# Loads of xn^T and x tied to one copy of the attention gradient, and two transposes of w_v moved behind the last dh1 transposes

## The chip, the cores and the metric

The kernel runs on one core of one Trainium2 chip. The time is device microseconds of one execution; several executions are timed and the median is given. The engines are named as in the profile: PE (TensorE matmul), PEld (its weight loads), DVE (VectorE), ACT (ScalarE), POOL (GpSimd) and SP (SyncE). SP issues the DMA transposes and the plain loads of one hardware queue (q1 in the profile), POOL issues plain copies through a software queue (q0). All matrices are bfloat16, all matmul sums fp32.

## What is computed

One transformer block (pre-LN linear attention with 32 heads of 20, then pre-LN SwiGLU) over 2048 tokens of width 640 and a hidden width of 1728, and its gradients with respect to x and all five weight matrices.

```python
def _A_ref(x, wqkv, wo):
    qkv = (x @ wqkv).reshape(B, S, 3, H, Dh).transpose(2, 0, 3, 1, 4)
    q, k, v = qkv[0], qkv[1], qkv[2]
    phi = lambda t: jnp.where(t > 0, t + 1, jnp.exp(t)) + 1e-6
    pq, pk = phi(q), phi(k)
    kv = jnp.einsum("bhsd,bhse->bhde", pk, v)
    z = jnp.einsum("bhsd->bhd", pk)
    num = jnp.einsum("bhqd,bhde->bhqe", pq, kv)
    den = jnp.einsum("bhqd,bhd->bhq", pq, z)[..., None] + 1e-6
    return (num / den).transpose(0, 2, 1, 3).reshape(B, S, D) @ wo
def _B_ref(x, w_gate, w_up, w_down):
    return (jax.nn.silu(x @ w_gate) * (x @ w_up)) @ w_down
h  = x + _A_ref(_layernorm(x), A_wqkv, A_wo)
h2 = h + _B_ref(_layernorm(h), B_w_gate, B_w_up, B_w_down)
out, vjp = jax.vjp(f, A_x, A_wqkv, A_wo, B_w_gate, B_w_up, B_w_down)
return (out, *vjp(grad_out))
```

## The kernel before

Tokens lie in 16 tiles of 128 rows ("token 14" below is tile 14 of 0 to 15), a width of 640 is five blocks of 128. The stages, with rough times in the span of the profile: layer norm and k, q (to 51 us), linear attention forward (to 139), the SwiGLU gradient in four column groups (to 436), the gradient through the second layer norm together with the gradient of the attention output (436 to 586), then the weight gradients of attention and dx (586 to 722), and the block's output (to the end).

The change sits in the stage from 436 to 586 us and in the code behind it. This stage is a loop over p (two tokens a turn) that works on three pairs of tokens at once. For the pair p the matmuls of d hn2 run (`ps_dhd`, `ps_dhc`, `ps_dha`). For the pair v = p - 1 the layer-norm gradient ends in dh1 (`ln_add`), and `tr_dh1` has SP transpose dh1 of each token by DMA into a buffer called `stg`, the odd token first. For the pair q = p - 2, with tokens u0 = 2q and u1 = 2q + 1, `dp_mm` multiplies that transposed dh1 with W2^T on PE into `ps_dp`, `dp_copy` copies it on ACT into `dq`, and DVE works on it. Three `stg` buffers are in turn: token 14's transpose writes the one that `dp_mm` of token 13 reads, and the first two row loads of pk (`pkr`) take the next turns.

In the turn p = 8, called `last` in the code, there is no pair left for d hn2, and PE fills its time with part sums of GT = dh1^T pq (`ps_gt`) for rows whose dh1 is ready. In the turn p = 9 only the pair 14 and 15 is left: `dp_mm(14)`, twelve `ps_gt` matmuls, `dp_mm(15)`. Then come two more blocks of `ps_gt`, `ps_dz`, the weight gradient `dwqk` (which reads x, normalised again in place in `hn`, there also called `xn_r`), `ps_dkvt`, `wk2` (which reads the transposed w_v), `ps_dk` (which reads xn^T, `xnT_r`) and `ps_dxn` (which reads the transposed w_q and w_k, and a ring of transposes).

The transposes on SP around that place are: five of w_o (`woT`, in turn 7), in turn 8 four column blocks of w_v by `tr_cols` into `wqkvT[:, 10 + j]`, then `tr_dh1` of tokens 15 and 14, then two more column blocks of w_v and ten of w_q and w_k. POOL, in turns 3, 5, 7 and 9, issues `load_xr4(c)`, which loads four tokens of x into `hn`, and after the loop four loads of xn^T, each of 640 KB, from the copy that the forward pass left in DRAM.

The stage stands in a `manual_schedule` of all engines, so the written order is the order of issue. `tc.issue_after(late)` in the part behind it only tells the scheduler where in the order an instruction may stand; it makes no semaphore. `late` is the `dp_copy` of the even token of the latest turn, in the end that of token 14. `wait_for(on, dmas)` (lines 216 to 219) adds a true dependency, so that the issuing queue waits on a semaphore until the instruction `on` has ended.

Of the kernel before, what the change touches and what calls it, by code (L numbers as in the profile page):

```python
# [20 lines left out]
def kernel(  # L21
# [8 lines left out]
    nc = tc.nc  # L30
# [18 lines left out]
    x_v = A_x.rearrange("b (t p) d -> p (b t) d", p=P)  # L49
# [16 lines left out]
    def row(ps):  # L66
        return ps[:, :, :320]

    def half(ap):
        return ap.rearrange("p (c n) -> p c n", c=2)  # L70
# [10 lines left out]
    scr_xnT = dram.tile([ST, P, DT, P], BF16, name="scr_xnT")  # L81
# [32 lines left out]
    HG = len(OH)  # L114
# [44 lines left out]
    def pool_load(out, in_):  # L159
        nc.gpsimd.dma_start(out=out, in_=in_)  # L160
# [54 lines left out]
    def wait_for(on, dmas):  # L215
        info = mybir.DependencyInfo(mybir.DependencyClass.Sync, mybir.DependencyReason.DATA)
        for dma in dmas:
            tc.add_manual_dep(dma.ins, on.ins.name, info, reason="paced")
# [266 lines left out]
    with tc.manual_schedule(engines={EngineType.PE, EngineType.DVE, EngineType.SP, EngineType.Pool}):  # L485
# [41 lines left out]
        hn = big.tile([P, ST, D], BF16, name="hn", tag="B")  # L527
# [410 lines left out]
    with tc.manual_schedule(engines=ALLE):  # L938
# [102 lines left out]
        def tr_cols(dst, src, c):  # L1041
            nc.sync.dma_start_transpose(out=dst.unsqueeze(1), in_=src[:, c:c + P])
# [3 lines left out]
        def get_wqkvT():  # L1046
            if not wqkvTs:
                wqkvTs.append(big.tile([P, 16, D], BF16, name="wqkvT", tag="B"))
            return wqkvTs[0]
# [19 lines left out]
        def dqv(t):  # L1069
            return dq[t // 8][:, t % 8, :]  # L1070
# [3 lines left out]
        def dp_mm(t):  # L1074
            pdp[t] = mm("ps_dp")
            d = dh1Ts.pop(t)
            mm_row(pdp[t], lambda i: d[:, i, :], lambda i, n0, n1: W2T[:, i, n0:n1], DT)

        def dp_copy(t):
            return nc.scalar.copy(out=half(dqv(t)), in_=row(pdp.pop(t)))  # L1080

        def dp_pr(t):
            tt(pr[:], dqv(t), pqs_tm[:, t, :], ALU.mult)
# [9 lines left out]
        def dp_end(t):  # L1093
            s = rw[t][:]
            tt(s, s, zb[:], ALU.mult)
            tt(dqv(t), dqv(t), s)
            tt(dqv(t), dqv(t), Eb[t][:], ALU.mult)
# [17 lines left out]
            nc.gpsimd.dma_start(out=out_6[j * P:min(j * P + P, F), :], in_=dwds.pop(j)[:min(P, F - j * P), :])  # L1115

        def load_xr4(c):
            nc.gpsimd.dma_start(out=hn[:, 4 * c:4 * c + 4, :], in_=x_v[:, 4 * c:4 * c + 4, :])

        gts = {}  # L1120

# [32 lines left out]
        for p in range(1, NPR + 2):  # L1154
            v, q = p - 1, p - 2
            e0, o0 = 2 * v, 2 * v + 1
            u0, u1 = 2 * q, 2 * q + 1
# [5 lines left out]
                for b in (*rws, *Ebs, pr):  # L1163
                    nc.gpsimd.memset(b[:, 0:1], 0.0)
            if last:
                for j in range(4):
                    tr_cols(get_wqkvT()[:, 10 + j, :], A_wqkv, 2 * D + OH[j])
            if run:
                load_pq(p)
# [59 lines left out]
                for i in range(3):  # L1229
                    gt_part(gts[i], i, ST - 2, ST)  # L1230
            if dpq:
                late = dp_copy(u0).ins
                dp_pr(u0)
                dp_mm(u1)
            if first:
# [40 lines left out]
            if run:  # L1276
                ln_mul(2 * p + 1)
            if p >= 3 and p % 2 == 1:
                with tc.issue_after(late):
                    load_xr4((p - 3) // 2)  # L1280
        dp_end(ST - 1)

    with tc.manual_schedule(engines={EngineType.SP, EngineType.DVE}):
# [3 lines left out]
        xnT_r = big.tile([P, ST, DT, P], BF16, name="xnT_r", tag="B")  # L1287
# [3 lines left out]
        def load_pk(t):  # L1291
            pkrs[t] = small.tile([P, D], BF16, name="pkr", tag="stg", bufs=3, padded_shape=[P, 7 * P])
            pool_store(pkrs[t][:], scr_pk_v[:, t, :])

        load_pk(0)
        load_pk(1)
        for j in range(4, HG):
            with tc.issue_after(last_dh1T):
                tr_cols(wqkvT[:, 10 + j, :], A_wqkv, 2 * D + OH[j])
        for k in (0, 1):  # L1300
# [1 line left out]
                with tc.issue_after(last_dh1T):  # L1302
                    tr_piece(wqkvT[:, 5 * k:5 * k + 5, :], A_wqkv[:, k * D:(k + 1) * D], i)
        for c in range(4):
            with tc.issue_after(late):
                pool_load(xnT_r[:, 4 * c:4 * c + 4], scr_xnT[4 * c:4 * c + 4].rearrange("t p k c -> p t k c"))

        GT = mat(2 * DT * D, DT, D)
        for i in range(DT):
# [51 lines left out]
        for r in range(4):  # L1361
            for ci, (n0, n1) in enumerate(NCH):
                for j in range(4):
                    t = 4 * r + j
# [302 lines left out]
```

## Time and profile before

| what | us |
|---|---|
| median of 3 runs | 792.43 |
| the runs | 790.3, 792.43, 800.54 |
| the profiled execution, its own time | 792.55 |
| its span, first to last instruction | 790.8 |
| PE busy in the span | 777.3 |
| DVE, ACT, POOL busy | 590.6, 347.7, 180.8 |

The span is what the engines' instructions cover; 1.75 us of the profiled execution's time lie around it. PE is busy for 98% of it, so the kernel is bounded by matmuls nearly everywhere, and what PE waits for is what can be had. The mean granted clock of TensorE is 0.994.

### The profile page before, as it was taken

To read this page: it belongs to the slowest core of one execution; us is meant where nothing else is said; L and a number is where in the kernel's file an instruction comes from. 1 tells how busy PE (TensorE), PEld (TensorE's weight loads), DVE (VectorE), ACT (ScalarE), POOL (GpSimd) and SP (SyncE) were. 2 spreads that over 40 slices of the span, in tenths; PEclk is the share of its full clock that TensorE was granted. 3 is DMA by queue.
4 is the path that set the end of the run, shared out by engine and by line. 5 is a ranking of instruction groups with operands and counts; after the bars stand their busy time and mean duration, and the time that the engine had idled before them with its cause. 6 is when DMAs were issued, how large, how long until landed. Compare 5 with 4: busy or idle time off the path is not lost.

```text
span 790.8 us, 14151 instructions
## 1 busy us (share of the span) xinstructions
PE 777.3 (98%) x5462; PEld 518.6 (66%) x5462; DVE 590.6 (75%) x1041; ACT 347.7 (44%) x545; POOL 180.8 (23%) x310
## 2 busy tenths in 40 slices
PE   9999999999999999999999999999969999999998
PEld 7676566556655665566666777777647777777776
DVE  7979988898697868776979379988843366634873
ACT  6962532762284145423831457766622133334010
POOL 4600037511201120012322222242201111123210
PEclk9999999999999999999999999999979999999999
DMA  9799999999679898892797699896984899999992
GB/s 261 163 238 302 201 226 261 274 243 229 190 164 220 183 228 191 215 241 80 158 232 232 212 221 241 224 274 123 204 193 113 151 149 183 177 172 315 236 203 89
DMA packets 288420, 162.37 MB, mean 205 GB/s; under 512 B 241548, under 2 KB 277197, under 8 KB 288352
## 3 DMA queue, kind: packets, MB, share of 16 engines
q1 hardware_dynamic: 269120, 101.25, 63.4%
q0 software_dynamic: 16608, 56.65, 24.0%
q10 hardware_dynamic: 2624, 3.56, 1.5%
q8 instruction: 43, 0.70, 0.4%
q14 instruction: 25, 0.20, 0.1%
HBM read 47.60 MB, written 53.66 MB: 128 GB/s over the span
## 4 chain that ended last, share of the span: by engine, by line
PE 90%; DVE 6%; DMA 3%; issue 1%; ACT 0%; POOL 0%; SPq 0%; ACTq 0%; DVEq 0%
PE ps_dxn L1430 8%; PE ps_wa L648 7%; PE pg L828 6%; PE pu L833 6%; PE ps_dwqk L1342 6%; PE ps_dm L422 5%; PE ps_qd L648 5%; PE ps_dha L991 5%; PE ps_oa L1507 4%; PE ps_kq L309 4%; PE ps_wc L648 3%; PE ps_dk L108 3%; PE ps_y L515 3%; PE ps_a L578 3%; PE ps_dw L684 3%; PE ps_dp L108 3%
## 5 line engine op out<-in xcount | busy, mean ns | idle before, releaser
L828 PE MATMUL pg<-wgu,hnT 128*128 128x448 bf16 (+1 forms) x320 | 64.1, 346 | 0.0
L833 PE MATMUL pu<-wgu,hnT 128*128 128x448 bf16 (+1 forms) x320 | 63.6, 346 | 0.0
L1430 PEld LDWEIGHTS <-ring 128*128 128x128 bf16 x480 | 46.9, 98 | 18.5 <-DMA ring<-dq 0.4
L1430 PE MATMUL ps_dxn<-wqkvT,ring 128*128 128x320 bf16 x320 | 51.3, 299 | 0.0
L833 PEld LDWEIGHTS <-hnT 128*128 128x128 bf16 x320 | 31.3, 98 | 27.1
L828 PEld LDWEIGHTS <-hnT 128*128 128x128 bf16 x320 | 31.3, 98 | 26.0
L422 PEld LDWEIGHTS <-dh2T 128*128 128x128 bf16 x320 | 31.0, 98 | 25.1
L422 PE MATMUL ps_dm<-wdT,dh2T 128*128 128x448 bf16 (+1 forms) x240 | 46.5, 344 | 0.0
L309 PE MATMUL ps_kq<-wqk,xnT 128*128 128x320 bf16 x320 | 44.8, 299 | 0.4 <-DMA xnT<-xn 0.4
L648 PEld LDWEIGHTS <-S 128*128 128x128 bf16 x320 | 30.9, 98 | 21.1 <-DVE dd L644 0.2
L849 ACT ACTIVATE dd<-pg 128x896 bf16<-128x896 f32 (+1 forms) x32 | 28.5, 891 | 28.9 <-PE pg L828 28.9
L309 PEld LDWEIGHTS <-xnT 128*128 128x128 bf16 x320 | 30.9, 98 | 12.9 <-DMA xnT<-xn 0.7
L1342 PEld LDWEIGHTS <-hn 128*128 128x128 bf16 x320 | 31.0, 98 | 12.1 <-issue 0.3
L873 POOL DMA_DIRECT2D scr_m<-m_s x16 | 12.2, 759 | 110.3 <-DVE m_s L860 110.3
L648 PE MATMUL ps_wa<-dd,hn 128*128 128x448 bf16 (+1 forms) x192 | 37.0, 346 | 0.0
L146 DVE CUSTOM_DVE_ANT_0 lb_a<-lb_dy,hn 128x640 bf16<-128x640 bf16 x16 | 13.2, 826 | 30.5 <-ACT lb_dy L144 30.5
L860 DVE TENSOR_TENSOR m_s<-m_s,dd 128x896 bf16<-128x896 bf16 (+1 forms) x32 | 19.3, 604 | 21.4 <-ACT m_s L853 21.4
L991 PEld LDWEIGHTS <-cols 128*128 128x128 bf16 x280 | 27.4, 98 | 10.6
L108 PE MATMUL ps_dp<-mats,stg 128*128 128x320 bf16 x160 | 25.7, 310 | 8.3 <-DMA stg<-dh 8.3
L644 DVE TENSOR_TENSOR dd<-dd 128x3584 bf16<-128x3584 bf16 (+1 forms) x16 | 31.3, 1954 | 3.0 <-PE ps_wc L648 3.0
L654 POOL DMA_DIRECT2D out_dram<-dwev x32 | 17.4, 545 | 68.8 <-DVE dwev L644 47.4
L144 ACT ACTIVATE lb_dy<-ps_dxn,rstd 128x640 bf16<-128x640 f32 x16 | 12.7, 794 | 45.1 <-PE ps_dxn L1430 45.1
(295 smaller groups left out, 1838.5 us busy)
## 6 DMA issues: line engine op xcount, KB each, us to landing
scr_dT<-stg SPq DMA_DIRECT2D x48, 224.0 KB, 2.8
cols<-scr_dT POOLq DMA_DIRECT2D x6, 1728.0 KB, 8.2
scr_m<-m_s POOLq DMA_DIRECT2D x12, 448.0 KB, 4.3
out_dram<-dwev POOLq DMA_DIRECT2D x30, 112.0 KB, 2.9
scr_pq<-pqa SPq DMA_DIRECT2D x4, 640.0 KB, 4.4
scr_xnT<-xnT SPq DMA_DIRECT2D x4, 640.0 KB, 5.4
scr_pk<-pk SPq DMA_DIRECT2D x4, 640.0 KB, 4.5
hn<-in_A_x_dram SPq DMA_DIRECT2D x4, 640.0 KB, 5.4
```

What stands on the lines that cost most here:

```text
L108: nc.tensor.matmul(ps[:, ci, :320], lhsT=lhs(k), rhs=rhs(k, *NCH[ci]), start=(start and k == 0), stop=(stop and k == n - 1))
L309: nc.tensor.matmul(ps[:, ci, :320], lhsT=xnT[:, t, k, :], rhs=wqk[:, k, w0 + n0:w0 + n1], start=(k == 0), stop=(k == DT - 1))
L422: nc.tensor.matmul(ps[:, c, :w], lhsT=dh2T[:, kt, (t + c) * P:(t + c + 1) * P], rhs=wdT[:, kt, o:o + w], start=(kt == 0), stop=(kt == DT - 1))
L644: nc.vector.tensor_tensor(out=out, in0=in0, in1=in1, op=op)
L648: nc.tensor.matmul(out, lhsT=lhs[:, t, :], rhs=rhs[:, t, :], start=(first and fresh and t == 0), stop=(t == 7), skip_group_check=not (firs ...
L828: nc.tensor.matmul(pg[:, c, :w], lhsT=hnT[:, kt, (t + c) * P:(t + c + 1) * P], rhs=wg[:, kt, 0:w], start=(kt == 0), stop=(kt == DT - 1))
L833: nc.tensor.matmul(pu[:, c, :w], lhsT=hnT[:, kt, (t + c) * P:(t + c + 1) * P], rhs=wg[:, kt, w:2 * w], start=(kt == 0), stop=(kt == DT - 1))
L849: sig = nc.scalar.activation(out=dg, in_=pg[:, :, :w], func=ACT.Sigmoid)
L991: nc.tensor.matmul(out, lhsT=lhs(k), rhs=rhs(k), start=(start and k == 0), stop=(k == HB - 1), skip_group_check=not start)
L1342: nc.tensor.matmul(ps[:, ci, :320], lhsT=xn_r[:, t, i * P:(i + 1) * P], rhs=dq[t // 8][:, t % 8, n0:n1] if which == 0 else dk[:, t, n0:n1] ...
L1430: nc.tensor.matmul(ps[:, ci, :320], lhsT=lhs[:, i, :], rhs=rhs[:, i, n0:n1], start=(k == 0 and i == 0), stop=(k == 2 and i == DT - 1))
L1507: nc.tensor.matmul(out, lhsT=lhs[:, k, :], rhs=rhs[:, k, :], start=(start and k == 0), stop=(stop and k == HK - 1), skip_group_check=not s ...
```

## The change

Two edits. The number of column blocks of w_v that are transposed ahead of the last two `tr_dh1` goes from four to two, and the other two follow behind them. And `load_xr4` and the four loads of xn^T get a true wait on the `dp_copy` that before was named for the scheduler alone: the four of xn^T and the last of x on that of token 14, the first three of x on those of tokens 2, 6 and 10.

```diff
         def load_xr4(c):
-            nc.gpsimd.dma_start(out=hn[:, 4 * c:4 * c + 4, :], in_=x_v[:, 4 * c:4 * c + 4, :])
+            return nc.gpsimd.dma_start(out=hn[:, 4 * c:4 * c + 4, :], in_=x_v[:, 4 * c:4 * c + 4, :])
...
             if last:
-                for j in range(4):
+                for j in range(2):
                     tr_cols(get_wqkvT()[:, 10 + j, :], A_wqkv, 2 * D + OH[j])
...
             if dpq:
-                late = dp_copy(u0).ins
+                late = dp_copy(u0)
                 dp_pr(u0)
                 dp_mm(u1)
...
             if p >= 3 and p % 2 == 1:
-                with tc.issue_after(late):
-                    load_xr4((p - 3) // 2)
+                with tc.issue_after(late.ins):
+                    wait_for(late, [load_xr4((p - 3) // 2)])
...
-        for j in range(4, HG):
+        for j in range(2, HG):
             with tc.issue_after(last_dh1T):
                 tr_cols(wqkvT[:, 10 + j, :], A_wqkv, 2 * D + OH[j])
...
         for c in range(4):
-            with tc.issue_after(late):
-                pool_load(xnT_r[:, 4 * c:4 * c + 4], scr_xnT[4 * c:4 * c + 4].rearrange("t p k c -> p t k c"))
+            with tc.issue_after(late.ins):
+                wait_for(late, [nc.gpsimd.dma_start(out=xnT_r[:, 4 * c:4 * c + 4],
+                                                    in_=scr_xnT[4 * c:4 * c + 4].rearrange("t p k c -> p t k c"))])
```

On SP, at the end of turn 7 and in turn 8, the order changes in one place (`stg<-dh` are the transposes of dh1 of tokens 15 and 14, `wqkvT` with 128x1x640 the column blocks of w_v, `mats<-in_A_wo_dram` those of w_o; the first row is tokens 13 and 12):

```order
 L1055 DMA_TRANSPOSE stg<-dh_1882 128x5x128 x2
 L931 DMA_TRANSPOSE mats<-in_A_wo_dram 128x5x128 x5
+L1042 DMA_TRANSPOSE wqkvT<-in_A_wqkv_dram 128x1x640 x2
+L1055 DMA_TRANSPOSE stg<-dh_1882 128x5x128 x2
 L1042 DMA_TRANSPOSE wqkvT<-in_A_wqkv_dram 128x1x640 x4
-L1055 DMA_TRANSPOSE stg<-dh_1882 128x5x128 x2
-L1042 DMA_TRANSPOSE wqkvT<-in_A_wqkv_dram 128x1x640 x2
```

Two column blocks have gone from ahead of the pair to behind it; nothing else on SP has moved.

POOL in turns 7 to 9 and behind the loop stands so before (`hn` the loads of x, the first of the two rows being that of turn 7; `xnT_r` those of xn^T; `pkr` the rows of pk; `scr_GT` the store of GT):

```order
L1118 DMA hn<-in_A_x_dram 128x4x640 [waits DMASW2_49,Activation_49]
L160 DMA xnT_r<-scr_xnT 128x4x640 [waits DMASW3_49,PE_49,Activation_49]
L1118 DMA hn<-in_A_x_dram 128x4x640 [waits DMASW4_49,DVE_49,Activation_49]
L160 DMA xnT_r<-scr_xnT 128x4x640 [waits DMASW5_49]
L160 DMA xnT_r<-scr_xnT 128x4x640 [waits DMASW6_49]
L163 DMA pkr<-scr_pk 128x640 [waits DMAHW3_49,DMASW7_49,PE_49]
L160 DMA xnT_r<-scr_xnT 128x4x640 [waits DMASW0_49]
L163 DMA pkr<-scr_pk 128x640 [waits DMAHW4_49,DMAHW0_49,DMAHW7_49,DMASW1_49,PE_49]
```

And so after the change, where the lines of the file behind line 1305 are one further down:

```order
L1118 DMA hn<-in_A_x_dram 128x4x640 [waits DMASW2_49,Activation_49]
L1118 DMA hn<-in_A_x_dram 128x4x640 [waits DMASW3_49,DVE_49,Activation_49]
L163 DMA pkr<-scr_pk 128x640 [waits DMAHW3_49,DMASW4_49,PE_49]
L163 DMA pkr<-scr_pk 128x640 [waits DMAHW4_49,DMAHW5_49,DMAHW0_49,DMAHW7_49,DMASW5_49,PE_49]
L1306 DMA xnT_r<-scr_xnT 128x4x640 [waits DMASW6_49]
L1306 DMA xnT_r<-scr_xnT 128x4x640 [waits DMASW7_49]
L1306 DMA xnT_r<-scr_xnT 128x4x640 [waits DMASW0_49]
L1306 DMA xnT_r<-scr_xnT 128x4x640 [waits DMASW1_49]
```

The last load of x now stands ahead of all loads of xn^T, both `pkr` rows stand ahead of them too, and the wait on ACT of that load of x, which POOL passes in order, also holds what follows it. On PE, DVE and ACT the order is the same before and after.

## Prediction

> **What bounds the kernel now.** I read the page's head and engine shares first, then the waits of PE, then the stages, then the chain of waits around the one long wait, then the order of time on SP and POOL there.
>
> ```profile
> span 790.8 us, 14151 instructions
> PE 777.3 (98%) x5462; PEld 518.6 (66%) x5462; DVE 590.6 (75%) x1041; ACT 347.7 (44%) x545; POOL 180.8 (23%) x310
> ```
>
> PE is idle for 790.8 - 777.3 = 13.5 us in all. More than that no change of waits alone can win, apart from matmuls that ran slowly. The waits of PE from 572 us to the end, and its busy time by stretch (length, then PE's busy time, the granted clock behind POOL's column):
>
> ```profile
> PE ps_dp L108 <- DMA stg<-dh: 8.3, 1, 8.3
> ...
> 430.00:571.00 141.00, 140.94 (x1050) 101.88 (x1049) 113.94 (x217) 87.62 (x171) 40.71 (x63) 1.00 0.88 212
> 571.00:580.00 9.00, 0.73 (x6) 0.32 (x4) 1.24 (x3) 0.00 (x0) 0.00 (x0) 0.66 1.06 315
> 627.00:725.00 98.00, 97.96 (x722) 70.36 (x721) 49.89 (x117) 31.15 (x52) 19.36 (x36) 1.00 0.98 187
> ```
>
> One wait holds 8.3 of those 13.5 us: `dp_mm(14)` waits for the transposed dh1. Before it (430 to 571) and behind it (627 to 725) PE has no gap to speak of. The chain of waits there (start, length, what):
>
> ```profile
> 567.12 12.67 DMA stg<-dh
> 579.79 0.05 issue
> 579.83 2.85 PE ps_dp L108 x10
> 582.68 2.41 PE ps_gt L1125 x12
> 585.09 1.36 PE ps_dp L108 x10
> 586.45 8.69 PE ps_gt L1125 x64
> ```
>
> The transpose of token 14 was issued at 567.12 and took 12.67 us. And the wait costs more than itself: ten `ps_dp` matmuls took 2.85 us right behind it and 1.36 us a little later, while the granted clock had been 0.66 in the stretch of the wait.
>
> Why it took so long is in the order of time on PE, ACT, SP and POOL (the second figure is the length of the whole row):
>
> ```profile
> 550.14 0.69 ACT L1080 CAST dq<-ps_dp 128x640 bf16<-128x640 f32 x1 [0.83 <-PE ps_dp L108]
> 565.15 1.52 PE L108 MATMUL ps_dp<-mats,stg 128*128 128x320 bf16 x10
> 566.51 5.05 PE L1125 MATMUL ps_gt<-pqs_tm,dh 128*128 128x320 bf16 x36
> 582.72 0.69 ACT L1080 CAST dq<-ps_dp 128x640 bf16<-128x640 f32 x1 [12.38 <-PE ps_dp L108]
> ...
> 549.55 2.83 SPq L1055 DMA_TRANSPOSE stg<-dh  x2
> 559.73 5.96 SPq L1042 DMA_TRANSPOSE wqkvT<-in_A_wqkv_dram  x4
> 565.79 9.53 SPq L1055 DMA_TRANSPOSE stg<-dh  x2
> 575.37 4.18 SPq L1042 DMA_TRANSPOSE wqkvT<-in_A_wqkv_dram  x2
> 579.60 14.09 SPq L931 DMA_TRANSPOSE wqkvT<-in_A_wqkv_dram  x10
> ...
> 549.48 1.24 POOL L1118 DMA_DIRECT2D hn<-in_A_x_dram  x1
> 561.48 0.76 POOL L160 DMA_DIRECT2D xnT_r<-scr_xnT  x1 [10.76 <-DVE pqs_tm L970]
> 562.43 0.75 POOL L1118 DMA_DIRECT2D hn<-in_A_x_dram  x1 [0.19 <-issue]
> 563.17 1.49 POOL L160 DMA_DIRECT2D xnT_r<-scr_xnT  x2
> 567.51 0.75 POOL L160 DMA_DIRECT2D xnT_r<-scr_xnT  x1
> ```
>
> The two dh1 transposes stand behind four column blocks of w_v, and beside them POOL has put five loads of 640 KB into the DMA engines, from 561.5 to 567.5. What the two queues moved from 570 to 577 us (packets, MB, share), and what SP's queue moved from 578 to 580, when the loads were done:
>
> ```profile
> q0 software_dynamic: 510, 2.28, 93.1%
> q1 hardware_dynamic: 496, 0.12, 9.3%
> ...
> q1 hardware_dynamic: 1985, 0.48, 113.4%
> ```
>
> Packet for packet the queues share evenly (510 to 496), but a packet of the loads has 2.28 MB / 510 = 4.5 KB and one of the transposes 0.25 KB. So the transposes got 71 packets per us beside the loads and 990 without them. The transposes of dh1 waited for the loads to end. From issue to landing (least, median, most) the pair 15 and 14 stands against the pair 13 and 12, issued at 549.55 beside one load of x, and against all sixteen:
>
> ```profile
> DMA to landing us min/median/max: 12.7/13.0/13.4
> ...
> DMA to landing us min/median/max: 6.0/6.0/6.1
> ...
> DMA to landing us min/median/max: 2.6/4.6/13.4
> ```
>
> **The change, part by part.**
>
> Two column blocks moved behind the pair. Four rows took 5.96 us on SP, 1.49 each, so `tr_dh1(15)` is issued at about 559.73 + 2 x 1.49 = 562.7 instead of 565.79. For token 14 this wins little: its buffer is the one that `dp_mm(13)` reads, and that ends at 565.15 + 1.52 = 566.67. So it is issued at about 566.8, 0.3 us earlier than now, but with an empty queue before it. The blocks themselves now come behind the pair, from 568 to about 574; `wk2` needs them at 606.4 less the gain (row below), 20 us later, so they cost nothing.
>
> The wait for `dp_copy(14)`. With it no large load is in flight between the load of x from turn 7 (issued at 549.48, now about 1.4 us later, since `dp_copy(10)` ends at 550.8) and the end of `dp_copy(14)`. The bounds for the transpose of token 14 are then 2.6 us (the fastest of the sixteen) and 6.1 us (the slowest of the pair that shared the engines with one load). It lands between 566.8 + 2.6 = 569.4 and 566.8 + 6.1 = 572.9. PE finishes its `ps_gt` at 566.51 + 5.05 = 571.56. What is left of the wait is 0 to 1.3 us. I take 0, since no load is beside it and even the median of 4.6 lands at 571.4. The gain is 579.83 - 571.56 = 8.27 us.
>
> The slow matmuls go with the wait: 2.85 - 1.36 = 1.49 us for the ten `ps_dp`, and for twelve `ps_gt` 2.41 - 12 x 8.69 / 64 = 0.78 us, together 2.27 us. The Trainium skill, page "TensorE: Matmul & The Clock Gate", Part 1, says that the array falls to half rate after an idle window of about 3.4 us and returns after a busy one of that length. By it the loss would be half of 3.4, 1.7 us, and the new time 0.6 us higher than by the rows; the trace's 2.27 us is used.
>
> What is late next. `dp_copy(14)` ends at 571.56 + 1.52 + 0.69 = 573.8. POOL then issues the last load of x, two `pkr` rows and four loads of xn^T, at 0.75 us each, up to about 579. Behind these on POOL stands the store of GT, which PE's work releases only 6 us later. The users, in the trace of before:
>
> ```profile
> 592.53 3.29 DVE L1358 TENSOR_SCALAR hn<-hn,mv,rstd 128x640 bf16<-128x640 bf16 x9
> 596.27 4.52 PE L1342 MATMUL ps_dwqk<-dq,hn 128*128 128x320 bf16 x32
> 606.41 1.05 PE L127 MATMUL ps_wk<-mats,wqkvT 128*128 128x120 bf16 x21
> 613.00 2.72 PE ps_dk L108 x20
> 627.13 4.08 PE ps_dxn L1430 x30
> ...
> DMA to landing us min/median/max: 6.4/7.1/10.0
> ```
>
> The last row is the landing of the four loads of x; the slowest, 10.0 us, would give 583.8. DVE normalises its first tile (token 12) at about 594.4 before, so 584.0 after, and PE reads it at 596.27 + 12 x 0.14 - 10.5 = 587.4. It is in time, with 3.6 us to spare on PE. The loads of xn^T, 2.6 MB at 2.28 MB per 7 us behind the 1.0 MB of x and `pkr`, end at about 576 + 11 = 587; `ps_dk` reads the first quarter at 613.0 - 10.5 = 602.5. No cost.
>
> The first three loads of x move by 0 to 1.4 us, in a stretch where PE is busy for 140.94 of 141 us. No cost, and no gain.
>
> **The sum.** The profiled execution took 792.55 us, 0.1 us off the median of 792.43, so the two serve alike. 792.55 - 8.27 - 2.27 = 782.0 us, 1.3% less.
>
> **The rivals.**
>
> A rest of the wait stays. If the transpose of token 14 shares the engines with what is left of the w_o and w_v transposes, its landing could be that of the pair 13 and 12 or somewhat more. At 6.1 us 1.3 us are left, at 10 us (the slowest load of x as the far bound) 566.8 + 10 - 571.56 = 5.2 us, and the slow matmuls come back in part. 783.3 to 789.5 us. Against it: from 562 to 571 only two column blocks and the pair itself are left on that queue.
>
> The change doesn't do what it says: the transpose is late for the queue's own sake, not for the loads. Then 12.67 us stay, the wait is only 0.3 us shorter, and the time is 792. Against it stands the rate of 71 against 990 packets per us.
>
> The loads are paid later, on the slower side. From 576 to 587 the same loads starve the ten transposes of w_q and w_k, behind which stand, in SP's order, the ring transposes and those of `wvk` that `ps_dxn` needs. If none of the ten moves before 587, they end at 587 + 14.1 = 601, two ring rows at 604, five of `wvk` at about 610, the first `ring<-dk` lands at about 614. `ps_dxn` starts at 627.1 - 10.5 = 616.6. Up to 2.6 us more are free, and the store of GT, which runs just then, takes about as much. From there each us that SP is later is a us of PE; to end slower than before it has to be 13 us later than this bound, to lose 2% 29 us. With 2 us paid the time is 784, with 13 us it is 792.5 and up. Against it: two or three of the ten are already issued before 576. The Trainium skill, page "DMA: Bandwidth & Descriptors", section "Issuing engines are not separate DMA queues", says that DMAs of all issuing engines run on the same 16 engines and interleave. By that rule the 3.6 MB cost the transposes as much as before, only later, and the trace agrees with its even share of 510 to 496 packets; whether anybody then waits is what decides between this rival and the forecast.
>
> **How the numbers follow.** The likeliest, the whole wait and the slow matmuls gone, gets 74 in 100: 779 to 783.5 us. The spread below 782 is that of the runs, whose fastest lies 2 us under the median, and 1 us for small idle pieces. A rest of the wait gets 11, no effect 5, the loads paid later 6, half of them past 2%. The last 4 are that far more goes than I can see. The range from 779 to 788 takes in the likeliest, most of the rest of the wait and the cheap end of the loads paid later, and leaves out about 15 in 100. A measurement of this kernel can tell about 2% from no change, 15.8 us. To be faster by that, all 13.5 us of PE's idle time and the slow matmuls would have to go: 4 in 100. Slower by over 2%: the 3 of the loads paid later. Within 2%: the other 93.
>
> **What would show it.** In the profile after, the wait of `ps_dp` for `stg<-dh` is gone from PE's list or under 1.5 us. The pair's transposes land within 6 us. The ten `ps_dp` of token 14 take 1.36 to 1.52 us and the granted clock stays at 1.00 there. The last load of x is issued at about 574 and the loads of xn^T behind it. `ps_dxn` starts some 10 us earlier, without a wait for `ring` or `wqkvT`. The prediction is wrong if the pair still takes over 10 us to land, if PE waits at `ps_dwqk`, `ps_dk` or `ps_dxn` for a load, or if a transpose that now runs beside the loads ends a chain.

## The result, and the profile after

| | before | with the change |
|---|---|---|
| median of 20 runs each, us | 796.32 | 785.01 |
| least and most, us | 789.96 to 806.02 | 782.42 to 801.98 |
| ratio, 95% interval | | 0.9871 [0.984, 0.9902] |
| profiled execution, its own time, us | 792.55 | 787.03 |

The change wins 1.3% (0.98 to 1.6%), about 10.3 us. The ratio is one of means, over the executions within 1.5% of the fastest of their kernel (17 of the 20 before, 16 of the 20 after). The page's head and PE's waits, longest first, after the change:

```profile
span 785.3 us, 14151 instructions
PE 777.4 (99%) x5462; PEld 519.1 (66%) x5462; DVE 590.9 (75%) x1041; ACT 347.7 (44%) x545; POOL 181.1 (23%) x310
...
PE ps_wc L648 <- DVE dd L644: 2.2, 1, 2.2
PE ps_warm L345 <- DVE ones L248: 1.1, 1, 1.1
PE ps_dp L108 <- DMA stg<-dh: 0.8, 1, 0.8
```

The 8.3 us of `ps_dp` are gone from the list. A wait of 0.8 us stands under the same name, and the chain of waits shows where:

```profile
555.25 7.28 DMA stg<-dh
562.53 0.05 issue
562.57 1.53 PE ps_dp L108 x10
564.10 6.52 PE ps_gt L1125 x48
570.62 1.36 PE ps_dp L108 x10
571.98 4.89 PE ps_gt L1125 x36
576.87 1.36 PE ps_dp L108 x10
578.23 1.63 PE ps_gt L1125 x12
579.86 1.36 PE ps_dp L108 x10
581.22 8.69 PE ps_gt L1125 x64
```

The first `ps_dp` row is token 12, whose transpose took 7.28 us: a new wait. Token 14 is the third `ps_dp` row, at 576.87. It follows the 36 `ps_gt` without a gap and takes 1.36 us, not 2.85, and the twelve `ps_gt` behind it take 1.63, not 2.41. The granted clock, in the column behind POOL's, stays at 1.00 where it had been 0.66, and the stage of `ps_dxn` is as full as before:

```profile
562.00:576.00 14.00, 13.43 (x99) 9.70 (x100) 12.99 (x30) 9.12 (x18) 0.00 (x0) 1.00 0.82 126
576.00:581.00 5.00, 5.00 (x39) 3.60 (x37) 2.45 (x5) 2.48 (x4) 1.74 (x3) 1.00 0.61 119
627.00:725.00 98.00, 98.00 (x724) 70.58 (x722) 53.88 (x121) 33.90 (x55) 22.70 (x42) 1.00 0.99 199
```

SP, then POOL in order of time, then the landing of the pair 15 and 14, and what SP's queue moved from 567 to 572, when the engines had almost nothing else:

```profile
566.56 3.44 SPq L1055 DMA_TRANSPOSE stg<-dh  x2
570.05 5.20 SPq L1042 DMA_TRANSPOSE wqkvT<-in_A_wqkv_dram  x4
575.29 28.78 SPq L931 DMA_TRANSPOSE wqkvT<-in_A_wqkv_dram  x10
614.95 1.23 SPq L1404 DMA_TRANSPOSE ring<-dk  x1
...
555.48 0.80 POOL L1118 DMA_DIRECT2D hn<-in_A_x_dram  x1 [1.21 <-DVE pqs_tm L970]
579.26 0.76 POOL L1118 DMA_DIRECT2D hn<-in_A_x_dram  x1 [22.98 <-ACT dq L1080]
581.09 2.99 POOL L1306 DMA_DIRECT2D xnT_r<-scr_xnT  x4
...
DMA to landing us min/median/max: 3.5/3.8/4.0
...
q1 hardware_dynamic: 2082, 0.51, 97.8%
```

POOL stands still for 23 us until ACT's copy of token 14 and only then issues the five loads. From 567 to 572 us the transposes move 2082 packets, 416 per us against 71 beside the loads (the 990 of the prediction, from 578 to 580 us, is not reached here), and the pair lands in 4.0 and 3.5 us instead of 13.4 and 12.7. The loads have not vanished: SP's ten transposes of w_q and w_k take 28.78 us beside them, 14.09 before. What that costs is a question for the runs below.

The profiled execution gains only 5.5 us, 792.55 to 787.03. The rest is chance in a stage that the change leaves alone: `ps_wc` of the SwiGLU gradient waits 2.2 us for DVE there, with slow matmuls behind it, and had no such wait in the profile before. To keep this out, the execution is cut at two places that the change does not touch: the first `ps_dp` matmul of token 10, and the first of the last 64 `ps_gt`. Before, these start at 548.58 and 586.28, after at 552.94 and 581.06:

| profile | until token 10 | between | from the last 64 `ps_gt` on |
|---|---|---|---|
| before | 548.6 | 37.70 | 204.5 |
| with the change | 552.9 | 28.12 | 204.2 |

The middle part, called the stretch below, loses 9.6 us. The last part is the same.

### The profile page after: what moved, and what is told of

It reads as the page before. It is cut to its first block, busy times and chain, and to the rows that moved or that the text cites. A ratio compares the mean times of both kernels' runs of the same rounds, so it can differ in the third digit from the quotient of the medians.

```text
span 785.3 us, 14151 instructions
## 1 busy us (share of the span) xinstructions
PE 777.4 (99%) x5462; PEld 519.1 (66%) x5462; DVE 590.9 (75%) x1041; ACT 347.7 (44%) x545; POOL 181.1 (23%) x310
## 4 chain that ended last, share of the span: by engine, by line
PE 86%; DVE 9%; DMA 3%; issue 1%; ACT 0%; SPq 0%; POOL 0%; DVEq 0%; ACTq 0%
PE ps_dxn L1431 8%; PE ps_wa L648 6%; PE ps_dwqk L1343 6%; PE ps_dm L422 6%; PE ps_qd L648 5%; PE ps_dha L991 5%; PE pg L828 4%; PE ps_oa L1508 4%; PE pu L833 4%; PE ps_kq L309 4%; PE ps_wc L648 3%; PE ps_y L515 3%; PE ps_dk L108 3%; PE ps_gt L1125 3%; PE ps_a L578 3%; PE ps_dp L108 3%
## 5 line engine op out<-in xcount | busy, mean ns | idle before, releaser
L309 PEld LDWEIGHTS <-xnT 128*128 128x128 bf16 x320 | 30.9, 98 | 12.7 <-DMA xnT<-xn 0.7
L146 DVE CUSTOM_DVE_ANT_0 lb_a<-lb_dy,hn 128x640 bf16<-128x640 bf16 x16 | 13.2, 826 | 30.3 <-ACT lb_dy L144 30.3
L138 POOL TENSOR_SCALAR lnv<-mv 128x1 f32<-128x1 f32 x32 | 12.0, 374 | 89.5 <-DVE mv L134 73.5
L144 ACT ACTIVATE lb_dy<-ps_dxn,rstd 128x640 bf16<-128x640 f32 x16 | 12.7, 794 | 44.9 <-PE ps_dxn L1431 44.9
```

The costliest lines, as they stand in the source:

```text
L309: nc.tensor.matmul(ps[:, ci, :320], lhsT=xnT[:, t, k, :], rhs=wqk[:, k, w0 + n0:w0 + n1], start=(k == 0), stop=(k == DT - 1))
```

## The experiments

Every run below is read in two ways: its ratio to the kernel before, and the stretch in its profile, which is free of the chance in the first part.

**The waits alone.** The number of blocks ahead goes back to four.

```diff
-                for j in range(2):
+                for j in range(4):
...
-        for j in range(2, HG):
+        for j in range(4, HG):
```

> The waits on the copy of token 14 alone; four column blocks of w_v stay ahead of the last two dh1 transposes. Stretch measured: from the first ps_dp matmul of token 10 to the first of the last 64 ps_gt matmuls, 37.9 us before and 28.1 with the whole change. Theory (the loads starve the transposes): with no load in flight the pair lands within 4 to 6 us although it is issued behind two more blocks, PE waits at most 1.5 us for token 14, the stretch is 28 to 30 us, the time about 1.1 to 1.3% under before. Rival (the place of the blocks counts): two blocks of 1.5 us more ahead hold the pair, the wait for token 14 stays at 3 us or more with the slow matmuls behind it, the stretch is 32 us or more.

Ratio 0.9945 [0.9908, 0.9983]; stretch 28.45 us, of which 1.1 us is token 12's wait. Token 14's rows on PE, the row ahead and those behind, and the landing of the pair:

```profile
570.16 5.05 PE L1125 MATMUL ps_gt<-pqs_tm,dh 128*128 128x320 bf16 x36
575.05 1.52 PE L108 MATMUL ps_dp<-mats,stg 128*128 128x320 bf16 x10
576.41 1.79 PE L1125 MATMUL ps_gt<-pqs_tm,dh 128*128 128x320 bf16 x12
...
DMA to landing us min/median/max: 2.6/2.6/2.6
```

No gap, although two more blocks stood ahead: the trace bears out the first theory, with the stretch in the forecast 28 to 30 us. The ratio is less than expected. In part that is the kernel before, which was quicker in this set (median 793.06 us, not 796.32); the median here, 785.76 us, is near the 785.01 of the changed kernel. The profile shows no further loss (204.4 us from the last 64 `ps_gt` on, as before), so whether the place of the two blocks costs some us in other executions stays open.

**The blocks alone.** The two ranges are changed as in the change, and no wait is added.

> Two column blocks moved behind the pair, no waits, so the five loads still go out while token 14's transpose is under way. Theory (the loads starve the transposes): token 14's transpose cannot be issued before dp_mm(13) ends and by then the loads run; it takes 8 us or more to land, PE waits 4 to 8 us, the slow matmuls stay, the stretch (37.9 before, 28.1 with the whole change) is 33 to 38 us, the time within 0.6% of before. Rival (the place of the blocks counts): the pair lands within 5 us and the stretch falls to 28 to 30 us without any wait on the loads.

Ratio 1.0007 [0.9962, 1.0052]; stretch 38.67 us, a little over what was expected and no better than before. The waits of PE, the loads on POOL, and the landing of the pair:

```profile
PE ps_dp L108 <- DMA stg<-dh: 8.5, 1, 8.5
...
567.30 0.76 POOL L160 DMA_DIRECT2D xnT_r<-scr_xnT  x1 [10.76 <-DVE pqs_tm L970]
568.25 0.75 POOL L1118 DMA_DIRECT2D hn<-in_A_x_dram  x1 [0.19 <-issue]
568.99 1.49 POOL L160 DMA_DIRECT2D xnT_r<-scr_xnT  x2
...
DMA to landing us min/median/max: 15.1/16.0/17.0
```

The pair takes even longer, since it is issued earlier and lands no earlier. Counted from the first matmul of token 10, token 14's transpose goes out at 16.6 us instead of 18.5 and lands at 31.7 instead of 31.2, while the loads go out at 12.9 us in both. The expectation that it cannot be issued before `dp_mm(13)` ends was wrong: it went out at 571.0, and `dp_mm(13)` ran from 571.13. From 576 to 583 us the loads moved 509 packets with 2.23 MB and SP's queue 422 with 0.10 MB, shared much as before the change. In the stretch, the waits do all the work of the two edits.

**Filling the wait.** The kernel before, with matmuls on constants in the place where PE waits; they are overwritten by `dp_mm(14)`.

```diff
             pdp[t] = mm("ps_dp")
+            if t == ST - 2:
+                for _ in range(56):
+                    nc.tensor.matmul(pdp[t][:, 0, :320], lhsT=ones[:], rhs=zb[:, 0:320], start=True, stop=True)
```

> The kernel before with 56 matmuls of 128x320 on constants put on PE just ahead of dp_mm(14), into its own accumulator, which it overwrites: 56 x 0.136 = 7.6 us of work inside the wait of 8.3 us, the transposes and loads untouched. Theory (the slow matmuls are a price of PE being idle): token 14's transpose lands as late as before, but the ten ps_dp take 1.4 to 1.5 us instead of 2.85 and the twelve ps_gt 1.6 instead of 2.4; the stretch falls from 37.9 by 2.3 to 35.6 us, the time by 0.3%. Rival (they are slow for what they wait for, the transposes landing piece by piece, or for the busy DMA engines): the ten ps_dp still take over 2.2 us, the stretch stays at 37 to 38 us.

Ratio 1.0007 [0.9968, 1.0045], too wide to tell 0.3%. The stretch fell to 35.16 us, 2.5 less than before:

```profile
573.64 7.77 PE L1078 MATMUL ps_dp<-zb,ones 128*128 128x320 bf16 x56
581.25 1.52 PE L108 MATMUL ps_dp<-mats,stg 128*128 128x320 bf16 x10
582.61 1.79 PE L1128 MATMUL ps_gt<-pqs_tm,dh 128*128 128x320 bf16 x12
```

With PE busy until the last moment the ten `ps_dp` and twelve `ps_gt` run as everywhere else. Their slowness was the price of idling, not of what they read. In this execution the pair landed in 8.0 to 8.7 us, so the fill, not the transpose, ended last, by about 1 us. The gain in the stretch therefore cannot be put down to the rows alone, and this run by itself does not rule out that data which have only just landed are slow to read. The profile after the change does: token 12's ten matmuls start right behind the landing of their data and take 1.53 us.

**The loads of xn^T twice.**

```diff
-        for c in range(4):
+        for c in (0, 1, 2, 3, 0, 1, 2, 3):
             with tc.issue_after(late.ins):
                 wait_for(late, [nc.gpsimd.dma_start(out=xnT_r[:, 4 * c:4 * c + 4],
```

> The changed kernel with the four loads of xn^T issued twice over, the second time with the same data to the same place: 2.6 MB more in the software queue behind the copy of token 14. It tests what the delayed loads still cost. Theory (they cost nothing as long as SP's row of transposes is through in time): the ten transposes of w_q and w_k, which end at 604 with the change, end 7 to 9 us later, ring<-dk of the first tile is issued at about 622 instead of 615, and ps_dxn, which started at 621.9, waits 2 to 6 us for it; the time is 0.3 to 0.8% above the changed kernel. Rival (nothing behind them waits): ps_dxn starts as early as with the change, no wait on PE over 0.5 us behind the last ps_gt, the time as the changed kernel.

Ratio 1.0105 [1.0034, 1.0175], some 2% above the changed kernel and more than expected; stretch 27.25 us. PE's waits from 600 to 650 us, and SP:

```profile
PE ps_dxn L1431 <- DMA wvk<-wvk: 3.0, 1, 3.0
PE ps_dxn L1431 <- DMA ring<-dk: 0.7, 1, 0.7
PE ps_dxn L1431 <- DMA ring<-dq: 0.5, 1, 0.5
...
573.21 39.25 SPq L931 DMA_TRANSPOSE wqkvT<-in_A_wqkv_dram  x10
622.77 1.23 SPq L1404 DMA_TRANSPOSE ring<-dk  x1
```

2.6 MB more in POOL's queue stretch SP's ten transposes from 28.78 to 39.25 us, and `ps_dxn` waits. So the way in which the delayed loads would be paid later is real, and the changed kernel stays on the right side of it by a few us in its two profiles. The profiled execution, 793.51 us, was the quickest of this kernel's ten and shows 9.4 us more behind the stretch. The other nine took 804.76 to 816.18 us, and the median of all ten is 807.69, so the loss is usually larger than the ratio tells; what they lost beyond that was not seen.

**Which load makes token 12 wait.** The changed kernel again, and three kernels beside it: one without waits on the first three loads of x, one that sends the load of turn 7 out with the last one, and one in which no load of x waits.

> The whole change again, as the measure for the three beside it on the same chip. 1.0 to 1.6% under before; in the stretch from the first ps_dp matmul of token 10 to the first of the last 64 ps_gt about 28.1 us, of which 0.8 us is a wait for the transpose of token 12 that the kernel before did not have.

```diff
                 with tc.issue_after(late.ins):
-                    wait_for(late, [load_xr4((p - 3) // 2)])
+                    ld = load_xr4((p - 3) // 2)
+                    if p > NPR:
+                        wait_for(late, [ld])
```

> The whole change, but the first three loads of x carry no wait, as before; only the last load of x and those of xn^T wait for token 14. Theory (the new 0.8 us wait of token 12 comes from the load of x in turn 7, which the wait moves from beside token 13's transpose to behind token 12's): that load goes out about 1.4 us earlier, token 12's transpose lands within 6.1 us, the wait is gone, the stretch is 27.3 us instead of 28.1. Rival (the wait is chance, as its slack before was only 0.2 us): the wait is there in this kernel as well, or in neither, and the stretch differs by less than 0.3 us.

```diff
                 with tc.issue_after(late.ins):
-                    wait_for(late, [load_xr4((p - 3) // 2)])
+                    for c in ([] if p == 7 else [2, 3] if p > NPR else [(p - 3) // 2]):
+                        wait_for(late, [load_xr4(c)])
```

> The whole change, but the load of x of turn 7 goes out with the last one, behind the copy of token 14, so that no load at all lies beside the last four dh1 transposes. Theory: token 12's transpose lands within 4 us, no wait of PE for dh1 transposes is left, the stretch is 27.3 us; the extra 640 KB behind token 14 delay the loads of xn^T by 2 us, which nobody needs for 15 us. Rival (it is only moved again): DVE's normalising of the tiles 8 to 11 waits for the load, and ps_dwqk on PE with it, 1 us or more.

```diff
                 with tc.issue_after(late.ins):
-                    wait_for(late, [load_xr4((p - 3) // 2)])
+                    load_xr4((p - 3) // 2)
```

> The whole change, but no load of x waits; only the four of xn^T do. The last load of x then goes out at about the place where the last two dh1 transposes are issued. Theory (the loads starve the transposes by their bytes): one load of 640 KB takes some 2 us of the engines, the pair lands 1 to 3 us later than with the whole change (6 to 7 us), PE waits 0 to 2.5 us for token 14; the stretch is 27.3 to 31 us. Rival (any large load in flight is enough to hold the pair): the pair takes 10 us or more and the stretch is 34 us or more.

| kernel | ratio, 95% interval | stretch | token 12's wait | landing of 15 and 14 |
|---|---|---|---|---|
| whole change | 0.9888 [0.9836, 0.9939] | 28.71 | 1.4 | 3.8 to 4.3 |
| first three of x free | 0.9887 [0.9833, 0.9942] | 27.17 | none | 2.6 to 3.7 |
| x of turn 7 late | 0.9888 [0.9837, 0.9939] | 27.17 | none | 2.6 to 3.1 |
| only xn^T waits | 0.9894 [0.9852, 0.9937] | 27.17 | none | 4.2 to 5.5 |

The stretch tells what the ratios cannot. In the two profiles of the changed kernel token 12 waits 0.8 and 1.4 us, and 1.1 with the waits alone. Where the load of turn 7 is not tied to `dp_copy(10)` no such wait is over 0.2 us. Token 12's transpose lands in 7.3 to 7.8 us in the three profiles with a wait of 0.8 us and more, in 6.1 to 6.7 where the load goes out ahead of it (six profiles, the next run's among them), and in 2.9 where the load comes late. Against the theory stands the kernel with the loads of xn^T twice: it has that tie, its transpose lands in 6.4 us, and it shows no wait. So the tie makes the wait likely, not certain. And one load of 640 KB beside the pair does it no harm (in the last kernel the last load of x goes out at 563.19, and PE does not wait), where five do; numbers between were not run.

The profile of the last kernel is of the slowest of its twelve executions, 798.91 us against a median of 789.30, and shows a wait behind the stretch that no profile of the changed kernel has:

```profile
PE ps_dxn L1431 <- DMA ring<-dk: 3.9, 1, 3.9
```

SP's ten transposes took 36.21 us there, against 25.5 to 30.3 in the five other profiles with the loads of xn^T once beside them, and the first `ring<-dk` went out only at 618.42. So the delayed loads can cost PE something without the 2.6 MB more. How often that happens was not measured.

**The loads of xn^T behind SP's transposes.** Each load of xn^T waits for the last transpose of w_k as well (`pieces`, what the last `tr_piece` returns); the first three loads of x are free.

```diff
+                ld = nc.gpsimd.dma_start(out=xnT_r[:, 4 * c:4 * c + 4],
+                                         in_=scr_xnT[4 * c:4 * c + 4].rearrange("t p k c -> p t k c"))
+                wait_for(late, [ld])
+                wait_for(pieces, [ld])
```

> The changed kernel without the waits on the first three loads of x (as in e4_x012_free), and the four loads of xn^T wait in addition for the last transpose of w_k, so that they no longer stand in the engines beside the ten transposes of w_q and w_k. It asks whether the delayed loads, which drew out SP's row of ten transposes to 28 to 30 us (14 us before), cost anything. Theory (with the whole change ps_dxn starts 4 us before it would have to wait, so nothing is lost in an ordinary execution): the ten transposes take 14 to 17 us, ring<-dk of the first tile is issued when its data are there, 10 us or more ahead of ps_dxn, the stretch stays at 27.2 us and the part behind it at 204.4 us; the time is that of e4_x012_free, 0.988 to 0.989 of before. Rival (the margin is eaten in many executions, which the profiles of ordinary ones don't show): the median falls by 2 us or more below that, to 0.986 or less, and the slowest runs are fewer. Third outcome, on the other side: the loads of xn^T now come too late and PE waits at ps_dk.

Ratio 0.9895 [0.9852, 0.9938]; stretch 27.43 us, 204.3 us behind it. SP:

```profile
572.76 15.25 SPq L931 DMA_TRANSPOSE wqkvT<-in_A_wqkv_dram  x10
...
606.58 1.27 SPq L1408 DMA_TRANSPOSE ring<-dk  x1
```

The ten transposes are back at 15.25 us and the first `ring<-dk` goes out 11.1 us ahead of `ps_dxn` (which starts at 617.65), not 6.8 as with the change, and the time stays. Whatever the delayed loads cost in some executions, it is too little or too rare for these times to show. None of these versions can be told from the changed kernel by its time.

## Why the prediction was right, and where it was not

**The wait for token 14.** Forecast: 0 to 1.3 us left, taken as 0. In the seven profiles with the loads of xn^T held back once, and in the one with them twice, it is 0. The landing of token 14 was given as 2.6 to 6.1 us and is 2.6 to 4.2; the pair's is 2.6 to 5.5.

**Its cause.** The queues share roughly packet for packet (510 to 496 before, 509 to 422 with the blocks alone), so the transposes get a twentieth of the bytes beside the loads. That it is the loads and not the place of the blocks, the blocks alone and the waits alone show, in opposite directions.

**When token 14's transpose is issued.** Here the sum had a wrong premise, and it did no harm. It let the transpose wait for `dp_mm(13)`, whose buffer it was said to write (so does the description of the kernel before), and therefore go out at 566.8 us, 0.3 us earlier than before. The rows of the transposes of 15 and 14 before and after, then a `pkr` load before, which takes a buffer of the same three:

```profile
L1055 SPq DMA_TRANSPOSE stg<-dh x2: 1224/4712/8200, 565.8 to 567.1; - x2
...
L1055 SPq DMA_TRANSPOSE stg<-dh x2: 1223/1663/2103, 566.6 to 567.9; - x2
...
566.97 0.55 POOL L163 DMA_DIRECT2D pkr<-scr_pk  x1 [2.31 <-PE ps_dp L108]
```

After the change it goes out at 567.9, over 2 us before `dp_mm(13)` begins (570.62 in the chain above). Before, at 567.1, it stood directly behind token 15's transpose, which held SP for 1.22 us; that `dp_mm(13)` had ended at 566.67 was chance. It is the first `pkr` load that `dp_mm(13)` releases, so token 14's buffer can only be the one that `dp_mm(12)` had read. The two blocks thus bring the transpose out 3.6 us earlier, not 0.3 (14.9 instead of 18.5 us behind the first matmul of token 10). It lands over 5 us ahead of its use, where the forecast left between 2 us of slack and 1.3 us of wait. The forecast of no wait was right with more room than its working had.

**The slow matmuls.** 2.27 us were taken from two rows. They are gone with the change, and filling the wait removes them without touching a transfer.

**The sum.** 8.27 + 2.27 = 10.54 us should have left the stretch, 37.70 to 27.16. Three kernels have 27.17. The changed kernel has 28.12 and 28.71, since one step failed.

**The step that failed**, by 0.8 to 1.4 us: "The first three loads of x move by 0 to 1.4 us, in a stretch where PE is busy for 140.94 of 141 us. No cost, and no gain." A busy PE was named as cover, but cover is the slack of the one transfer that PE needs next. Before, token 12's transpose was issued at 550.9 and landed 6.1 us later, 0.2 us ahead of its use, the weight load at 557.14:

```profile
557.14 1.32 PEld L108 LDWEIGHTS <-stg 128*128 128x128 bf16 x10
```

The load of turn 7 was issued 1.4 us ahead of it before (549.48) and 0.2 us behind it after (555.48 against 555.25): token 13, which had time, now lands in 4.1 us, and token 12, which had none, in 7.28. The rows for this were all in the profile before. By one of the prediction's own signs of being wrong, "if a transpose that now runs beside the loads ends a chain", it is wrong in this one place, by 0.8 to 1.4 of some 10 us.

**What is late next.** SP's lag was bounded by a first `ring<-dk` landing at 614 for a `ps_dxn` at 616.6. In the profile after, which runs some 5 us later than that reckoning, it is issued at 614.95, lands 2.7 us later, and `ps_dxn` starts at 621.90, without a wait. With 2.6 MB more it does wait, and in the slowest execution of the kernel in which only xn^T waits it does too. The forecast that nobody waits held in both profiles of the changed kernel, with some 4 us to spare.

**The time itself.** 782.0 us was worked out against a profile of 792.55; the twenty runs of before have a median of 796.32, so 785.01 lies 3 us above the figure while the ratio is the forecast one. The runs differ in the part ahead of the change: 548.6 to 556.7 us in eleven profiles, with a wait of `ps_wc` for DVE of 0 to 6.4 us. The sum also took the wait and the slow matmuls from one profile. The quickest executions of the two kernels lie only 7.5 us apart (789.96 and 782.42), and in the run that fills the wait token 14's transpose landed about 1.4 us sooner beside the same loads. So the stall before the change is probably shorter in some executions than in the one that the sum goes by; no profile of such an execution was kept, and this stays open.

## What to carry to other kernels

A bulk load that nobody needs soon can be held back by one semaphore wait, and that is worth as much as the stall of the small transfer it would have drowned, plus the slow matmuls behind the stall. Before it is held back to a certain point, look at what is in flight at that point too: each transfer issued within a few us of the new place has its own slack, and the one with the least decides. And when runs scatter by more than the gain, cut the profile at two marks around the change and compare the piece between.

## What was not expected of the hardware

The slow matmuls cost 2.27 us behind an idle time of 8.27 us, but about 2.8 us behind one of 8.54 in the run with the blocks alone (38.67 - 27.17 - 8.54, less 0.15 by which token 12 was late there), whose rows are 2.85 and 3.15 us long against 1.52 and 1.79. Behind the short waits of token 12, up to 1.4 us, there was no such price: its ten matmuls took 1.53 us each time. The Trainium skill, page "TensorE: Matmul & The Clock Gate", Part 1, agrees with the latter, since it needs an idle window of about 3.4 us; half of one, 1.7 us, as an estimate of the price is too low by both measurements.
